# Stores of squared activations moved three products back in one issue queue, and three loads moved ahead

## The chip, the cores and the metric

The kernel runs on one core of a Trainium2 chip. The core has a matrix engine (TensorE, PE in the profile), which reads its operands from on-chip memory (SBUF) and adds into eight banks of a second memory (PSUM), and three engines for elementwise work: VectorE (DVE), ScalarE (ACT) and GpSimd (POOL). SyncE (SP) computes nothing: its queue issues the transfers (DMA) between SBUF and main memory. An engine takes its instructions strictly in order and stops at the first one that has to wait for another engine or for a transfer. The metric is the device time of one execution in microseconds.

## The reference

Attention with a threshold, and behind it a feed-forward network:

```
scores = q k^T / 8;  keep scores >= rowmax - tau;  softmax;  x = weights v      # 8 x 8 heads, 576 x 64
h = maximum(x @ w_in, 0)            # x 4608 x 512, w_in 512 x 2048
out = (h * h) @ w_out               # w_out 2048 x 512
```

All results are float32. The change lies in the feed-forward part, in its first layer `h * h`.

## The kernel before

**Three stages.** The attention comes first (to about 492 us) and leaves x transposed in main memory. The first layer (to about 881 us) computes squares g = max(x w_in, 0)^2 and stores them in main memory (`gT`). The output layer loads them again and multiplies by w_out. Tokens come in nine steps of 512.

**Products.** Both layers multiply with a scheme of seven products for eight, used twice: an outer index m runs over `OUTER = (1, 2, 6, 7, 4, 5, 3)` and, in each m, seven inner products, so that a pass has 49 products. I number them 0 to 48 in a pass; m = 1 has 0 to 6, m = 2 has 7 to 13, and so on. Each product goes into a PSUM bank and is then added into running sums: by DVE alone, or by DVE into one of six places (tag `t`) and from there by POOL (`add`, `final`). The m = 2, 4, 5 and 3 each finish four tiles of g (tag `o`, a ring of eight places); I call them block 2, 4, 5 and 3. So a place of `o` is written again two blocks later.

**Passes.** There are nine passes over the 49 products (`PASSES`): pass 0 for step 0, passes 1 to 6 for the pairs of steps (1, 2), (3, 4), (5, 6) with half of the columns each, passes 7 and 8 for steps 7 and 8. Passes 1 to 6 work on 256 tokens at once (L1000), the others on 128 (L817).

**What goes on beside the products.** `tick` (L1041) follows every product; what it emits stands in the engines' queues in that order, though an engine that is free may run ahead. It does, in this order:
- `chain_out`: weight chains for the second layer. A chain loads 256 KB of raw blocks of w_out (L1298), takes four differences of them on POOL six to nine products later (`minus`, L122) and stores the result (L1303) ten products behind its load. Chains begin at products 6, 12, 18, 24, 36 and 45 of each pass, and use two SBUF places in turn: a chain's load waits until the store of the chain before the last has landed.
- `before_x` (L921), in passes 0, 2, 4 and 6: loads the next steps' x from main memory (`load_x`, L838), by the table `BEFORE_X`: `(i, at): (part, slot)`, i counting the m's in their order and `at` the products in it. The slots are those of the steps now in work, each free once PE has read it for the last time; slot `None` is a place among x's sums. The first sum of the new x (from product 21 on) subtracts what lies in `None` from slot 2: ACT copies one operand into PSUM (`sum_v`, L856), and DVE subtracts (L122) one product later.
- `squares_due`: when a tile of g has been complete for six products (ten for block 3), ACT makes its Relu and its Square (L969, L970) and, at once, `square` puts its stores into SP's queue: one of 256 KB (L973) in a pass over one step, two of 128 KB (L976) in a pass over two.

SP's queue thus holds chain loads and stores, x loads and stores of squares in the order in which `tick` emits them. At the start of pass 8 the output layer's first loads (L1082) join it, and reloads of weights (L1225) follow.

Of the kernel before, what the change touches and what calls it, by code (L numbers as in the profile page):

```python
# [48 lines left out]
def kernel(  # L49
# [25 lines left out]
    nc = tc.nc  # L75
# [9 lines left out]
    BANK = 512  # L85
# [9 lines left out]
    gT = [[dram.tile([P, BANK], FP32, name=f"g{n}_{j}") for j in range(16)] for n in range(NSTEP)]  # L95
# [79 lines left out]
    raws, parts, asked_for = {}, {}, set()  # L175
# [336 lines left out]
    for g in range(2, 2 * len(pairs)):  # L512
        two, x = divmod(g - 4, 4)
# [300 lines left out]
    def by_tiles(to, lhs, rhs, start, stop):  # L814

        for cols in (ds(0, HALF), ds(HALF, HALF)):
            nc.tensor.matmul(to[cols], lhs[:, cols], rhs, start=start, stop=stop, skip_group_check=True)  # L817
# [68 lines left out]
    def part_x(steps, k, m, count=None):  # L886

        of = slice((steps[0] + 1) % 2, (steps[0] + 1) % 2 + len(steps))
        ms = slice(m - 1, m - 1 + count) if count else m - 1
        if k in (1, 7, 2, 3):  # L890
            return places_x[:, of, ms, k in (2, 3), k in (7, 3), :]
        return sums_x[:, of, (5, 6, 4).index(k), ms, :]
# [8 lines left out]
    def outer_x(steps, op, o, x, y):  # L901

        return [lambda n=n: sum_v(op, slot_x(n, o), slot_x(n, x), slot_x(n, y)) for n in steps]
# [9 lines left out]
    def ask_x(steps, m, slot):  # L913

        (part,) = [(a, c) for a, c in XPARTS if AT_B[a][c] == m]
        for n in steps:
            load_x(n, [part], slot_x(n, slot))

    BEFORE_X = {(1, 0): (1, 1), (1, 6): (7, None), (2, 0): (3, 2), (3, 6): (2, 2), (6, 0): (3, 5)}

    def before_x(steps, i, at):  # L921

        if (i, at) in BEFORE_X:
            ask_x(steps, *BEFORE_X[i, at])
        turned_ = lambda: outer_x(steps, minus, 6, 2, None)
# [23 lines left out]
        }  # L949
        return work.get((i, at), list)()  # L950

    LATER = {3: 4}
    waiting, half_made = deque(), []

    def advance_x():
# [7 lines left out]
    squares, clock = deque(), {"n": 0}  # L963
    def hidden_bank():
        return banks.tile([P, BANK], FP32, tag="b", bufs=6, name="ph")

    def square(n, j, o):

        nc.scalar.activation(out=o, in_=o, func=AF.Relu)  # L969
        nc.scalar.activation(out=o, in_=o, func=AF.Square)  # L970
        steps, h = n
        if h is None:
            nc.sync.dma_start(out=gT[steps[0]][j][:, :].rearrange("p (k t) -> p k t", k=4), in_=o)  # L973
            return
        for s_, step in enumerate(steps):
            nc.sync.dma_start(  # L976
                out=gT[step][j][:, ds(h * BANK // 2, BANK // 2)].rearrange("p (k t) -> p k t", k=2),
                in_=o.rearrange("p (k s) t -> p k s t", s=2)[:, :, s_, :],
            )

    def squares_due(wait):

        if squares and squares[0][0] + wait <= clock["n"]:
            square(*squares.popleft()[1:])

    def hidden_layer(n, also):

        steps, h = n
        of = prepared.pop(steps[0], None)
        tile4 = lambda tag, bufs: hid.tile([P, 4, NQ], FP32, tag=tag, bufs=bufs)  # L990
        bank = lambda: hidden_bank()[:, :].rearrange("p (k t) -> p k t", k=4)
        temp = lambda name: tile4("t", 6)
        U2, U3 = {}, {}

        for m in OUTER:

            def product(to, k, more):
                if h is not None:
                    for j in range(2):
                        nc.tensor.matmul(  # L1000
                            to[:, 2 * j : 2 * j + 2, :], W_IN[m, k][:, ts(2 * h + j, P)], part_x(steps, k, m),
                            start=(not more and j == 0), stop=True, skip_group_check=True,
                        )
                    return
                x = of[k][:, m - 1, :] if of else part_x(steps, k, m)[:, 0, :]
                for j in range(4):
                    by_tiles(to[:, j, :], W_IN[m, k][:, ts(j, P)], x, not more and j == 0, True)

            def add(to, c, other, more, t=None):

                if other is None:
                    plus(nc.vector, to, c, more)
                else:
                    plus(nc.gpsimd, to, t, more)

            def final(ab, c, other):
                if m == 1:
                    U2[ab] = tile4("u", 12)
                    if other is None:
                        nc.scalar.copy(U2[ab], c)  # L1020
                    else:
                        plus(nc.vector, U2[ab], c, other)
                    return
                t = None
                if other is not None:
                    t = temp("t")
                    plus(nc.vector, t, c, other)
                if m == 6:
                    add(U2[ab], c, other, U2[ab], t)
                elif m == 7:  # L1030
                    U3[ab] = tile4("u", 12)
                    add(U3[ab], c, other, U2[ab], t)
                else:
                    o = tile4("o", 8)
                    add(o, c, other, U3[ab] if m in (4, 5) else U2[ab], t)
                    if m == 5:
                        add(U2[ab], c, other, U2[ab], t)
                    row, col = {2: (0, 0), 4: (1, 0), 5: (1, 1), 3: (0, 1)}[m]
                    squares.append((clock["n"] + LATER.get(m, 0), n, 4 * (2 * row + ab[0]) + 2 * col + ab[1], o))

            def tick(at):  # L1041
                clock["n"] += 1
                also(m, at)
                squares_due(6)

            inner(product, copy, temp, bank, final, tick)


# [130 lines left out]
    with tc.manual_schedule():  # L1179
# [127 lines left out]
        for n, (steps, h) in enumerate(PASSES):  # L1307
# [14 lines left out]
            def also(m, at):  # L1322
                i = OUTER.index(m)
                convert_out(n, 7 * i + at)
                chain_out(n, 7 * i + at)
                if ahead:
                    waiting.extend(before_x(ahead, i, at))
                if 0 < n < 8 and h != 1:
                    waiting.extend(within_x(group, i, at))
                advance_x()  # L1330
                if not last:
                    return
                spread(work.get(i, []), at)
                reload_due(7 * i + at)

            hidden_layer((steps, h), also)
        for n in range(NSTEP):
            more = n + 1 < NSTEP

            def work_of(i):  # L1340

                work = [] if i == 6 else inner_sums(n, OUTER[i + 1])
                if (n, i) == (0, 0):
                    work += outer_sums(0, 6, (1, 2)) + outer_sums(0, 5, (4,)) + outer_sums(0, 6, (4,))
                if (n, i) == (0, 1):
                    work += outer_sums(0, 7, (1, 2, 4))
                if (n, i) == (0, 2):
                    work += outer_sums(0, 3, (1, 2, 4))
                if more and i == 4:
                    work += outer_sums(n + 1, 5) + outer_sums(n + 1, 7, (7, 1))  # L1350
                if more and i == 5:
                    work += outer_sums(n + 1, 6) + outer_sums(n + 1, 7, (2, 4))
                if more and i == 6:
                    work += outer_sums(n + 1, 3) + inner_sums(n + 1, 1)
                return work

            def also(m, at):
                i = OUTER.index(m)
                if n == 0:
                    reload_due(49 + 7 * i + at)  # L1360
                if n == 0 and (i, at) in ((2, 0), (3, 0)):
                    load_g(1, [(m_, k) for m_ in ((7,) if i == 2 else (4, 1, 2)) for k in K_ORDER])
                if n and more and (i, at) == (0, 0):
                    load_g(n + 1, [(m_, k) for m_ in KINDS[0:2] for k in K_ORDER])
                if at == 0:
                    work[0] = work_of(i)
                spread(work[0], at)
                if at > 4:
                    squares_due(-max(LATER.values()))
                if at == 2:  # L1370
                    ask()
                if at == 6:
                    if n and more and i == 0:
                        load_g(n + 1, [(7, k) for k in K_ORDER])
                    if n and more and i == 1:
                        load_g(n + 1, [(4, k) for k in K_ORDER])

            work = [None]
            output_layer(n, also)
# [37 lines left out]
```

## Time and profile before

| what | us |
|---|---|
| three runs, median (lowest to highest) | 1272.59 (1271.4 to 1273.39) |
| the profiled execution, its own time | 1272.82 |
| span of that execution, first to last instruction | 1271.0 |
| PE busy | 1249.6 |
| DVE, POOL, ACT busy | 989.3, 983.2, 844.4 |
| first layer, nine passes | about 491.9 to 881.5 |

The page's times are of one execution on the chip. A row of a timeline gives start, duration, engine, line, operation, output and input, how many instructions it joins and, in brackets, how long the engine stood idle before it and what ended that. Rows of SPq are transfers being issued; they land some microseconds later. A row of windows gives a stretch, its length, and busy time (with the count of instructions) of PE, weight loads, DVE, ACT and POOL, then the clock granted to PE as a share of the full one, the busy share of the transfer engines, and GB/s.

### The profile page before, as it was taken

Reading aid. Unit: us, or ns where it says so; the run is one execution under the profiler, and the core shown is the slowest. Engines: PE = TensorE matmul, PEld = TensorE weight load, DVE = VectorE, ACT = ScalarE, POOL = GpSimd, SP = SyncE. Lnnn points to the kernel's source line nnn. Section 1 sums busy time; section 2 is a strip of 40 time slices with the busy share of each in tenths; the row PEclk is TensorE's granted clock in tenths of the full one; section 3 lists DMA queues with packets and bytes.
Section 4 is the critical chain, followed back from the end, with each engine's and each line's share of the span. In section 5 each row is a group of like instructions: output and inputs, shape, how many; then the busy total and the mean of one; then the engine's idle time right before and its main releaser. Section 6 shows DMA issues by size and latency. Waiting matters only on the chain.

```text
span 1271.0 us, 55420 instructions
## 1 busy us (share of the span) xinstructions
PE 1249.6 (98%) x22991; PEld 1093.1 (86%) x22991; DVE 989.3 (78%) x2385; ACT 844.4 (66%) x1536; POOL 983.2 (77%) x1070
## 2 busy tenths in 40 slices
PE   8999999999999999999999999999999999999998
PEld 5777777777777778987888888999999999999998
DVE  6999999999999996886887878867746654665463
ACT  6999999999999994665765866675524432443240
POOL 3989998877776543987897988868787878787776
PEclk9999999999999999999999999999999999999999
DMA  7666676434333323658768768679755225522511
GB/s 184 149 166 157 168 193 187 118 93 105 89 83 87 79 60 99 199 161 230 200 190 226 217 172 232 192 260 374 278 163 168 78 97 163 168 69 101 167 36 35
DMA packets 291450, 196.81 MB, mean 155 GB/s; under 512 B 100096, under 2 KB 252160, under 8 KB 291200
## 3 DMA queue, kind: packets, MB, share of 16 engines
q1 hardware_dynamic: 289888, 192.87, 53.0%
q8 instruction: 181, 2.97, 1.0%
q14 instruction: 69, 0.57, 0.1%
q10 hardware_dynamic: 1312, 0.41, 0.1%
HBM read 120.85 MB, written 72.35 MB: 152 GB/s over the span
## 4 chain that ended last, share of the span: by engine, by line
PE 74%; DMA 2%; POOL 2%; ACT 1%; issue 1%; DVE 1%; SPq 0%; DVEq 0%; ACTq 0%; POOLq 0%
PE po L817 30%; PE ph L1000 14%; PE ph L817 10%; PE sc L560 7%; PE sc L458 6%; PE pt L402 4%; POOL arena L125 1%; PE sc L541 1%; PE sc L422 1%; DMA w<-arena 1%; DMA arena<-w 1%; POOL arena L122 1%; ACT arena L969 1%; PE sc L402 0%; DVE arena L125 0%
## 5 line engine op out<-in xcount | busy, mean ns | idle before, releaser
L125 POOL TENSOR_TENSOR arena<-arena 128x512 f32<-128x512 f32 (+1 forms) x314 | 378.7, 1224 | 118.6 <-DVE arena L125 105.2
L817 PE MATMUL po<-wall,arena 128*64 128x128 f32 x7056 | 385.5, 273 | 0.8 <-ACT arena L812 0.8
L817 PEld LDWEIGHTS po<-wall,arena 128*64 128x64 f32 x7056 | 385.2, 137 | 1.0 <-ACT arena L812 1.0
L125 DVE TENSOR_TENSOR arena<-ph,arena 128x512 f32<-128x512 f32 x378 | 254.9, 689 | 78.1 <-PE ph L1000 31.9
L122 POOL TENSOR_TENSOR arena<-arena 128x128 f32<-128x128 f32 (+1 forms) x322 | 265.9, 827 | 30.9 <-DMA arena<-w 14.4
L1000 PE MATMUL ph<-arena,wall 128*128 128x256 f32 x1176 | 257.7, 381 | 2.8 <-DVE arena L125 2.6
L1000 PEld LDWEIGHTS ph<-arena,wall 128*128 128x128 f32 x1176 | 223.6, 191 | 36.8 <-DVE arena L125 6.3
L125 DVE TENSOR_TENSOR arena<-po,arena 128x128 f32<-128x128 f32 x378 | 108.0, 290 | 159.4 <-PE po L817 153.9
L491 DVE SCALAR_TENSOR_TENSOR arena<-arena 128x576 f32<-128x576 f32 x288 | 226.0, 821 | 0.4 <-ACT arena L486 0.4
L486 ACT ACTIVATE arena<-arena 128x576 f32<-128x576 f32 x288 | 213.5, 779 | 13.2 <-DVE arena L476 13.1
L476 DVE TENSOR_SCALAR_CACHE_REDUCE arena<-sc 128x576 f32<-128x576 f32 x288 | 203.4, 753 | 15.9 <-issue 5.7
L856 ACT COPY c<-arena 128x512 f32<-128x512 f32 (+1 forms) x295 | 168.8, 578 | 69.9 <-DVE arena L122 37.5
L458 PE MATMUL sc<-arena 64*64 64x512 f32 (+1 forms) x2304 | 178.1, 413 | 5.8 <-ACT arena L551 1.4
L560 PE MATMUL sc<-arena 64*64 64x128 f32 (+1 forms) x5760 | 165.8, 261 | 1.1 <-ACT arena L551 0.5
L122 DVE TENSOR_TENSOR arena<-arena,c 128x512 f32<-128x512 f32 x235 | 154.5, 666 | 12.0 <-ACT c L856 6.6
L560 PEld LDWEIGHTS sc<-arena 64*64 64x64 f32 x5760 | 150.4, 133 | 4.8 <-issue 1.0
L551 ACT COPY arena<-pt 128x1024 f32<-128x1024 f32 x143 | 144.9, 1013 | 3.3 <-PE pt L402 2.6
L458 PEld LDWEIGHTS sc<-arena 64*64 64x64 f32 x2304 | 76.6, 133 | 70.4 <-issue 44.2
L812 ACT COPY arena<-po 128x128 f32<-128x128 f32 x63 | 16.6, 264 | 177.6 <-PE po L817 174.8
L817 PE MATMUL ph<-arena,wall 128*64 128x128 f32 x2352 | 129.2, 273 | 0.6 <-DVE arena L709 0.6
L817 PEld LDWEIGHTS ph<-arena,wall 128*64 128x64 f32 x2352 | 128.3, 137 | 1.4 <-issue 1.0
L483 POOL TENSOR_SCALAR arena<-arena,tau_p 128x2 f32<-128x2 f32 x144 | 83.3, 579 | 55.6 <-DVE arena L476 42.2
(55 smaller groups left out, 1140.4 us busy)
## 6 DMA issues: line engine op xcount, KB each, us to landing
arena<-g SPq DMA_DIRECT2D x144, 256.0 KB, 5.0
g<-arena SPq DMA_DIRECT2D x192, 128.0 KB, 2.9
w<-arena SPq DMA_DIRECT2D x60, 256.0 KB, 3.2
wall<-w SPq DMA_DIRECT2D x49, 256.0 KB, 5.2
g<-arena SPq DMA_DIRECT2D x48, 256.0 KB, 4.2
arena<-w SPq DMA_DIRECT2D x44, 256.0 KB, 3.4
arena<-in_v_dram SPq DMA_DIRECT2D x32, 288.0 KB, 4.0
out_dram<-arena SPq DMA_DIRECT2D x70, 128.0 KB, 2.7
```

Of the source, the lines that this page charges most:

```text
L122: e.tensor_tensor(out=out, in0=x, in1=y, op=ALU.subtract)
L125: e.tensor_tensor(out=out, in0=x, in1=y, op=ALU.add)
L458: made = nc.tensor.matmul(sc[at, ds(to, count)], lhs, kT[rows, ds(at_k, count)], start=True, stop=True)
L476: made = nc.vector.tensor_scalar(out=s[:, j, :], in0=sc[:, ds(at, S)], scalar1=1.0, scalar2=None, op0=ALU.mult, op1=ALU.min, accum_out=nmx ...
L483: nc.gpsimd.tensor_scalar(out=thr, in0=nmx, scalar1=tau_p[:, :], scalar2=None, op0=ALU.add)
L486: nc.scalar.activation(out=w[:, :, j, :], in_=of(j), func=AF.Exp, bias=nmx[:, j : j + 1], scale=-1.0)
L491: nc.vector.scalar_tensor_tensor(out=w[:, :, j, :], in0=of(j), scalar=thr[:, j : j + 1], in1=w[:, :, j, :], op0=ALU.is_le, op1=ALU.mult, a ...
L551: touch(kind, copy_by(joined(to), whole(pt, 0, count)), at, 2 * BANK, m)
L560: made = nc.tensor.matmul(sc[ds(u * D, D), ds(5 * j * BANK + row, count)], loaded_v[i][rows, (c - (u != j)) % CH, :], wT[m][rows, ds(weigh ...
L817: nc.tensor.matmul(to[cols], lhs[:, cols], rhs, start=start, stop=stop, skip_group_check=True)
L856: nc.scalar.copy(c, y)
L1000: nc.tensor.matmul(to[:, 2 * j : 2 * j + 2, :], W_IN[m, k][:, ts(2 * h + j, P)], part_x(steps, k, m), start=(not more and j == 0), stop=Tr ...
```

## The change

The stores of squares are no longer emitted with the square. They are kept in a list with the clock (the count of products) at the square, and `stores_due(LATE)`, called in every tick behind `also` and ahead of `squares_due`, emits those that are three products old. Before a place of `o` is written again, any store still kept for it is emitted first. In the output layer the clock goes on, with stores one product old in step 0, and all that are left after it. Three entries of `BEFORE_X` move: part 1 into slot 1 from the tick of product 7 to that of product 6, part 7 into `None` from 13 to 11, part 3 into slot 2 from 14 to 13.

```diff
-    BEFORE_X = {(1, 0): (1, 1), (1, 6): (7, None), (2, 0): (3, 2), (3, 6): (2, 2), (6, 0): (3, 5)}
+    BEFORE_X = {(0, 6): (1, 1), (1, 4): (7, None), (1, 6): (3, 2), (3, 6): (2, 2), (6, 0): (3, 5)}
...
-    LATER = {3: 4}
+    LATER, LATE = {3: 4}, 3
...
         if h is None:
-            nc.sync.dma_start(out=gT[steps[0]][j][:, :].rearrange("p (k t) -> p k t", k=4), in_=o)
+            to = gT[steps[0]][j][:, :].rearrange("p (k t) -> p k t", k=4)
+            kept.append((clock["n"], made_number(o), [(to, o)]))
             return
+        parts = []
         for s_, step in enumerate(steps):
...
+            parts.append((to, o.rearrange("p (k s) t -> p k s t", s=2)[:, :, s_, :]))
+        kept.append((clock["n"], made_number(o), parts))
...
+    def stores_due(wait, before=0):
+
+        while kept and (kept[0][0] + wait <= clock["n"] or kept[0][1] < before):
+            for to, from_ in kept.popleft()[2]:
+                nc.sync.dma_start(out=to, in_=from_)
...
+                    stores_due(LATE, len(hidden_made) - 7)
                     o = tile4("o", 8)
+                    hidden_made.append(o)
...
                 also(m, at)
+                stores_due(LATE)
                 squares_due(6)
...
+                clock["n"] += 1
+                stores_due(1 if n == 0 else 0)
```

In SP's queue of passes 1 to 6 this gives the following order (stores of squares by their block; a block has eight stores of 128 KB, so "2 of block 2" is one tile):

```
before: chain load 12, x loads, 2 of block 2, chain store 16, 4 of block 2, chain load 18, 2 of block 2, chain store 22, chain load 24
after:  chain load 12, x loads, chain store 16, chain load 18, 8 of block 2, chain store 22, chain load 24
```

The numbers are the products at which they are emitted. The order of instructions on PE, DVE, ACT and POOL stays as it was.

More of the change, by code (lines that the diff above doesn't have):

```diff
@@ L972, in square, with made_number @@
         if h is None:
-            nc.sync.dma_start(out=gT[steps[0]][j][:, :].rearrange("p (k t) -> p k t", k=4), in_=o)
+            to = gT[steps[0]][j][:, :].rearrange("p (k t) -> p k t", k=4)
+            kept.append((clock["n"], made_number(o), [(to, o)]))
             return
+        parts = []
         for s_, step in enumerate(steps):
[L976 to L979, printed above, removed]
+            to = gT[step][j][:, ds(h * BANK // 2, BANK // 2)].rearrange("p (k t) -> p k t", k=2)
+            parts.append((to, o.rearrange("p (k s) t -> p k s t", s=2)[:, :, s_, :]))
+        kept.append((clock["n"], made_number(o), parts))
+    hidden_made, kept = [], deque()
+    def made_number(o):
+        return next(i for i, x in enumerate(hidden_made) if x is o)
+    def stores_due(wait, before=0):
+        while kept and (kept[0][0] + wait <= clock["n"] or kept[0][1] < before):
+            for to, from_ in kept.popleft()[2]:
+                nc.sync.dma_start(out=to, in_=from_)
     def squares_due(wait):
```

## The prediction

> **What bounds the kernel now.** First the page's busy times, then the busy times of the nine passes of the hidden layer by window, then the waits of PE and of SP's queue, last the timelines around the one long wait. The waits of SP's queue are those between 540 and 950 us.
>
> ```profile
> span 1271.0 us, 55420 instructions
> PE 1249.6 (98%) x22991; PEld 1093.1 (86%) x22991; DVE 989.3 (78%) x2385; ACT 844.4 (66%) x1536; POOL 983.2 (77%) x1070
> ...
> 534.80:577.60 42.80, 42.80 (x197) 37.08 (x197) 34.96 (x57) 30.13 (x55) 38.10 (x47) 1.00 0.64 184
> 577.60:624.50 46.90, 44.33 (x198) 38.22 (x197) 32.77 (x50) 27.67 (x51) 37.11 (x47) 0.96 0.71 198
> 667.30:709.90 42.60, 42.60 (x197) 37.14 (x197) 32.54 (x51) 27.09 (x50) 35.43 (x45) 1.00 0.77 213
> ...
> PE ph L1000 <- DVE arena L125: 2.6, 1, 2.6
> PE po L817 <- ACT arena L812: 0.8, 1, 0.8
> ...
> SPq L1303 <- POOL arena L122: 62.0, 29, 4.3
> SPq L973 <- ACT arena L970: 20.2, 15, 9.0
> SPq L976 <- ACT arena L970: 14.0, 24, 2.0
> ```
>
> PE is busy 98% of the span. The windows are passes 1, 2 and 4: a pass over two steps takes 42.6 to 42.8 us and PE is never idle in it, but pass 2 takes 46.9. That is all this change can win: 46.9 - 42.8 = 4.1 us, 0.32%. SP's queue waits 62.0 us for POOL (results of the weight chains, L1303) and 34.2 us for ACT (squares to be stored, L973, L976). POOL, not PE, is the engine with the next least room: 38.1 of 42.8 us.
>
> ```profile
> 586.30 0.46 SPq L1298 DMA_DIRECT2D arena<-w  x1
> ...
> 593.41 0.49 SPq L1298 DMA_DIRECT2D arena<-w  x1
> 594.00 2.04 SPq L838 DMA_DIRECT2D arena<-xT  x4
> ...
> 599.77 1.31 ACT L856 COPY c<-arena 128x512 f32<-128x512 f32 x2 [2.52 <-DMA arena<-xT]
> ...
> 601.31 0.69 DVE L122 TENSOR_TENSOR arena<-arena,c 128x512 f32<-128x512 f32 x1 [3.03 <-DMA arena<-xT]
> ...
> 602.66 29.58 PE L1000 MATMUL ph<-arena,wall 128*128 128x256 f32 x126 [2.57 <-DVE arena L125]
> ...
> 602.00:604.00 2.00, 1.34 (x3) 1.17 (x4) 1.87 (x5) 0.00 (x0) 1.74 (x4) 0.60 0.55 163
> 604.00:606.00 2.00, 2.00 (x6) 1.55 (x6) 1.31 (x3) 0.00 (x0) 0.77 (x1) 0.54 0.54 149
> ...
> 885.00:890.00 5.00, 4.50 (x82) 4.50 (x84) 3.50 (x9) 4.08 (x9) 3.95 (x4) 1.00 1.04 390
> ```
>
> The stall of pass 2: four x loads go out at 594.0; the sum of x (L122) starts at 601.31, when the third has landed; DVE's next sums free the bank that PE waits for, and PE resumes at 602.66 after 2.57 us. The granted clock then falls to 0.60 and 0.54 for four microseconds, which is the rest of the 4.1. PE resumes 1.35 us after the sum starts, so PE would not have stopped had the sum started 2.57 us sooner, at 598.74: that is 21.1 us into the pass.
>
> **The change, part by part.** No instruction is added or removed on any engine, and the order on PE, DVE, ACT and POOL is the old one. What moves is the order in SP's queue, which issues one after the other and stops at the first that has to wait. So no place in the program makes a store "later" by three products in time; it makes it later by what now stands ahead of it. The price of a place is
>
> ```profile
> 570.56 6.53 SPq L976 DMA_DIRECT2D g<-arena  x12
> ```
>
> 6.53 / 12 = 0.54 us.
>
> (a) The x loads. In pass 2 the old queue has, behind the chain load at 586.30 (L1298, product 6), 12 issues and then the load that the sum needs. The new one has 14: the loads for slot 1 and for the free place (`None`) move up, but the two stores of block 3's first square, ahead of 586.30 before, now come behind it. The third of the four loads (some 595.1 in the row of 594.00) is thus two places later, not sooner: 1.1 us at the price above, against which stand the waits for ACT that go. The rows bound it: had SP no wait at all from 586.30 on, 15 x 0.54 = 8.1 us puts it at 594.4, 0.7 sooner; at the old pace, (595.1 - 586.3) / 13 = 0.68, it goes out 10.2 us behind, 1.4 later. I take +0.5 for the stall, a little over the middle, since the waits of SP that a landing transfer ends stay. In passes 4 and 6 the same two places are lost:
>
> ```profile
> 687.84 0.68 DVE L122 TENSOR_TENSOR arena<-arena,c 128x512 f32<-128x512 f32 x1
> ...
> 773.38 0.69 DVE L122 TENSOR_TENSOR arena<-arena,c 128x512 f32<-128x512 f32 x1
> ```
>
> Passes 4 and 6 begin at 667.3 and 752.6, so PE's limits are 688.4 and 773.7: room of 0.6 and 0.3. A load that landed at most at these starts, 1.1 later, costs PE up to 0.5 and 0.8. I take 0.5 for both together, since the landings themselves may be earlier.
>
> (b) The stores of block 2's squares. They were spread around the chain load of product 18; now all eight stand between that load and the chain store of product 22.
>
> ```profile
> 690.13 0.36 SPq L1298 DMA_DIRECT2D arena<-w  x1
> 690.58 1.00 SPq L976 DMA_DIRECT2D g<-arena  x2
> 691.63 0.54 SPq L1303 DMA_DIRECT2D w<-arena  x1
> 694.85 0.36 SPq L1298 DMA_DIRECT2D arena<-w  x1
> ...
> 697.25 0.99 POOL L122 TENSOR_TENSOR arena<-arena 128x128 f32<-128x128 f32 x2
> ...
> 732.53 0.97 SPq L976 DMA_DIRECT2D g<-arena  x2
> ...
> 775.92 0.97 SPq L976 DMA_DIRECT2D g<-arena  x2
> ...
> 740.06 0.46 POOL L122 TENSOR_TENSOR arena<-arena 128x128 f32<-128x128 f32 x1 [0.64 <-DMA arena<-w]
> ```
>
> The chain load of product 24 writes the place that the store of product 22 reads, so it waits for that store to land (694.85 behind 691.63), and POOL begins with it as soon as it is there (second half of the row 697.25; idle 0.64 in pass 5). Of the old stores four were hidden in the wait for the chain store of product 16, and two cost 1.0. Now eight cost 8 x 0.54 = 4.3, and the wait ahead of 690.13 stands empty: POOL's sums come 3.3 us later in passes 4, 5 and 6. What is late next is DVE: it writes each partial sum into one of six places that POOL must have read, and this reserve is already used up at the end of a pass:
>
> ```profile
> 578.24 0.69 DVE L125 TENSOR_TENSOR arena<-ph,arena 128x512 f32<-128x512 f32 x1 [0.67 <-POOL arena L125]
> ...
> 710.76 0.69 DVE L125 TENSOR_TENSOR arena<-ph,arena 128x512 f32<-128x512 f32 x1 [0.20 <-POOL arena L125]
> ...
> 753.02 0.69 DVE L125 TENSOR_TENSOR arena<-ph,arena 128x512 f32<-128x512 f32 x1 [0.45 <-POOL arena L125]
> ...
> 796.08 0.69 DVE L125 TENSOR_TENSOR arena<-ph,arena 128x512 f32<-128x512 f32 x1 [0.23 <-POOL arena L125]
> ```
>
> This sum and two more (three at 0.69, which overlap a little: 1.9 us) come ahead of the sixth product of the next pass, which begins 5 x 0.873 = 4.4 us into it. With 3.3 added: 710.76 + 3.3 + 1.9 = 716.0 against 709.9 + 4.4 = 714.3, a stall of 1.7; 758.2 against 757.0, 1.2; 801.3 against 799.7, 1.6. Together 4.5 us. In pass 1 the store of product 22 waited for POOL anyway:
>
> ```profile
> 555.24 0.44 SPq L1298 DMA_DIRECT2D arena<-w  x1
> ...
> 558.10 0.36 SPq L1303 DMA_DIRECT2D w<-arena  x1
> ```
>
> 2.9 us, against 0.45 + 4.3 = 4.8 now: 1.9 later, 578.24 + 1.9 + 1.9 = 582.0 against 582.0, no stall. I take pass 3 like pass 1, and pass 2 at nothing, since its own stall gives POOL time. The ends for (b): 0, if POOL turns out to have room, and 4.5 plus the clock.
>
> (c) The clock. A wait of 2.57 us cost 1.5 more by the clock; one of 0.8 (row 885: clock 1.00) cost nothing. The new stalls of 1.2 to 1.7 lie between, nearer to 0.8: I take nothing, with 4.5 (three times 1.5) as the other end. "TensorE: Matmul & The Clock Gate" of the Trainium skill (section Why this matters for your kernels) would have the clock hold through gaps under some 3 us; by that the new stalls cost no clock, as I take it, but the rows 602 and 604 show it falling after 2.57, so the measurement decides and the other end stays.
>
> (d) Stores of blocks 4, 5 and 3. Block 4's keep their place behind the chain load of product 36. Block 5's go behind the chain store of product 46, and their places are rewritten by block 2 of the next pass: 581.36 (that store) + 8 x 0.54 lands well before product 59; if that cover went, POOL would wait. At the end of pass 7 three stores go behind 16 loads; POOL is not short of time there. The output layer's stores go one product later; PE's only wait there (0.8) is for ACT. All at nothing.
>
> Sum: 0.5 + 0.5 + 4.5 = 5.5 us on the profiled execution's 1272.82, so 1278.3; the median of the three runs lies 0.2 below that execution, so 1278.0 us.
>
> **The rivals.** (1) Faster: SP, no longer held by squares, issues the loads 2.6 us sooner, the sum of pass 2 starts by 598.74, and POOL's reserve hides (b). For it: 34.2 us of waits for ACT; against it: the third load's two lost places. The price is the whole 4.1: 1272.6 - 4.1 = 1268.5. "DMA: Bandwidth & Descriptors" (Rules for kernel authors) speaks for this rival: issue the DMA early, wait late. Here the early issue holds for two of the three places only. (2) Nothing much: (b) is hidden and (a) alone counts, 1272.6 + 1.0 = 1273.6. For it: DVE's waits for POOL are under 0.7 and PE shows none. (3) Worse: (b) as reckoned, and the clock falls after each of the three stalls: 1278.0 + 4.5 = 1282.5.
>
> **How the numbers follow.** My forecast 0.52, (1) 0.20, (2) 0.14, (3) 0.14. Two runs can be told apart from about 0.2%, 2.5 us. Faster 0.20, same 0.12 (most of rival 2), slower 0.68. The likeliest case alone reaches from 1274 (half of b) to 1282; the range reaches up to rival 3 and down to half of the stall of pass 2 gone: 1270.0 to 1284.0.
>
> **What would show it.** In the profile after: in passes 4 to 6 eight stores in a row between the chain load of product 18 and the chain store of product 22, POOL idle for a chain load some 3 us longer at product 30, DVE waiting for POOL at the ends of these passes, and PE waits of 1 to 2 us just into passes 5, 6 and 7, where there are none now. Pass 2 keeps a wait of about 3 us. Wrong, if pass 2 takes 43 us or the passes after it stay at 42.7.

## The result, and the profile after

The changed kernel takes 1291.55 us (median, 1289.25 to 1291.79) against 1272.34 for the kernel before: a ratio of 1.0147, 95% interval 1.0129 to 1.0164. It is slower, as forecast, but by 19.2 us and not by 5.4; 1291.55 lies above the range.

Views of the changed kernel: the span from its page, the windows of passes 2, 4 and 6 with two microseconds inside pass 2, and the waits between 530 and 900 us (total, times, longest).

```profile
span 1287.4 us, 55410 instructions
...
575.20:625.70 50.50, 45.97 (x197) 39.06 (x197) 33.54 (x52) 28.22 (x50) 38.15 (x47) 0.93 0.69 192
604.00:606.00 2.00, 2.00 (x6) 1.57 (x5) 1.10 (x2) 0.00 (x0) 1.92 (x4) 0.50 1.04 306
668.50:718.10 49.60, 45.76 (x198) 38.94 (x197) 33.06 (x51) 28.23 (x51) 37.64 (x47) 0.93 0.69 192
761.60:811.00 49.40, 45.14 (x200) 37.84 (x200) 33.14 (x52) 28.79 (x51) 38.01 (x47) 0.97 0.71 197
...
POOL arena L122 <- DMA arena<-w: 32.8, 14, 4.5
DVE arena L122 <- DMA arena<-xT: 13.4, 3, 4.9
PE ph L1012 <- DVE arena L125: 12.6, 5, 4.4
DVE arena L125 <- POOL arena L125: 7.1, 7, 1.8
```

The same two lines of POOL and DVE in the kernel before:

```profile
POOL arena L122 <- DMA arena<-w: 14.1, 11, 3.4
...
DVE arena L125 <- POOL arena L125: 1.8, 5, 0.7
```

The loss sits in the three passes that load the next x. Pass 2 grew from 46.9 to 50.5 us, pass 4 from 42.6 to 49.6, pass 6 (as long as pass 4 before) to 49.4: 3.6 + 7.0 + 6.8 = 17.4 us. DVE waits in each of them for an x load (13.4 us in three waits), PE waits 12.6 us for DVE where it waited 2.6, and after each long wait the granted clock stands at 0.50, for 6.8 us in passes 2 and 4 and for 3.4 us in pass 6, which makes most of the other 7.4. (The spans differ by 16.4 us: passes 5 and 7 add some 1.4, and in this execution the first layer begins 2.5 us earlier than in that of before.)

The chain that leads there is best read in SP's queue, in passes 3 and 4 (L1313 chain load, L1318 chain store, L991 stores of squares, L838 x loads). First the changed kernel:

```profile
646.21 5.21 SPq L991 DMA_DIRECT2D g<-arena  x8
651.51 0.44 SPq L1318 DMA_DIRECT2D w<-arena  x1
654.47 0.36 SPq L1313 DMA_DIRECT2D arena<-w  x1
...
657.63 0.45 POOL L122 TENSOR_TENSOR arena<-arena 128x128 f32<-128x128 f32 x1 [3.20 <-DVE arena L122]
...
670.51 1.53 POOL L122 TENSOR_TENSOR arena<-arena 128x128 f32<-128x128 f32 x3
...
673.71 0.36 SPq L1318 DMA_DIRECT2D w<-arena  x1
674.17 5.58 SPq L991 DMA_DIRECT2D g<-arena  x8
679.84 0.68 SPq L1318 DMA_DIRECT2D w<-arena  x1
680.57 0.50 SPq L1313 DMA_DIRECT2D arena<-w  x1
...
688.72 0.49 SPq L1313 DMA_DIRECT2D arena<-w  x1
689.32 2.12 SPq L838 DMA_DIRECT2D arena<-xT  x4
...
695.08 1.22 PE L1012 MATMUL ph<-arena,wall 128*128 128x256 f32 x2 [3.72 <-DVE arena L125]
```

and the kernel before (L1298 chain load, L1303 chain store, L976 stores of squares):

```profile
648.04 0.46 SPq L1303 DMA_DIRECT2D w<-arena  x1
650.79 0.36 SPq L1298 DMA_DIRECT2D arena<-w  x1
...
666.98 1.53 POOL L122 TENSOR_TENSOR arena<-arena 128x128 f32<-128x128 f32 x3
...
670.17 0.36 SPq L1303 DMA_DIRECT2D w<-arena  x1
670.63 4.07 SPq L976 DMA_DIRECT2D g<-arena  x4
674.79 0.42 SPq L1303 DMA_DIRECT2D w<-arena  x1
675.30 0.52 SPq L1298 DMA_DIRECT2D arena<-w  x1
...
680.40 0.53 SPq L1298 DMA_DIRECT2D arena<-w  x1
680.97 4.47 SPq L838 DMA_DIRECT2D arena<-xT  x8
```

Passes 3 and 4 begin 1.2 us later in the changed kernel, so 1.2 is to be taken off each difference. The eight stores of block 2 at 646.21 put chain store 22 from 648.04 to 651.51 and chain load 24 from 650.79 to 654.47 (2.5 later within the pass). POOL stands 3.20 us before its difference at 657.63; the row names DVE as the releaser, but that chain load landed at 657.57. POOL is still 2.3 us late at the pass end (670.51), so chain store 46 goes out 2.3 later (673.71). Behind it now stand the eight stores of block 5 (674.17), where four stood before, and chain store 6 with chain load 6 is 4.1 later (680.57). Then come block 3's stores, chain load 12 is 7.1 later (688.72), and behind it the load of slot 2 begins at 689.32. In the kernel before it is the second half of the eight at 680.97, from 683.2 on (680.97 + 4 x 4.47 / 8): 4.9 us sooner within the pass. Of these 4.9 us, 2.3 are POOL's lateness (block 2), some 1.7 come with the four more stores between chain stores 46 and 6 (block 5), and the last 0.9 between chain load 6 and the load of slot 2, where two more stores of block 3 now stand. PE stops for 3.72 us.

### The profile page after: what moved, and what is told of

It is laid out like the page before. It is cut to its first block, busy times and chain, and to the rows that moved or that the text cites. A ratio compares the mean times of both kernels' runs of the same rounds, so it can differ in the third digit from the quotient of the medians.

```text
span 1287.4 us, 55410 instructions
## 1 busy us (share of the span) xinstructions
PE 1256.9 (98%) x22991; PEld 1095.7 (85%) x22991; DVE 990.1 (77%) x2385; ACT 845.0 (66%) x1536; POOL 981.7 (76%) x1070
## 5 line engine op out<-in xcount | busy, mean ns | idle before, releaser
L125 POOL TENSOR_TENSOR arena<-arena 128x512 f32<-128x512 f32 (+1 forms) x314 | 378.1, 1222 | 109.8 <-DVE arena L125 90.1
L125 DVE TENSOR_TENSOR arena<-ph,arena 128x512 f32<-128x512 f32 x378 | 255.6, 689 | 84.9 <-PE ph L1012 31.3
L1012 PE MATMUL ph<-arena,wall 128*128 128x256 f32 x1176 | 265.5, 388 | 13.3 <-DVE arena L125 12.6
L1012 PEld LDWEIGHTS ph<-arena,wall 128*128 128x128 f32 x1176 | 226.6, 194 | 51.9 <-DVE arena L125 19.6
L125 DVE TENSOR_TENSOR arena<-po,arena 128x128 f32<-128x128 f32 x378 | 107.9, 289 | 159.5 <-PE po L817 154.0
L122 DVE TENSOR_TENSOR arena<-arena,c 128x512 f32<-128x512 f32 x235 | 154.6, 666 | 23.5 <-DMA arena<-xT 13.4
```

The lines of the kernel that those rows point to most:

```text
L122: e.tensor_tensor(out=out, in0=x, in1=y, op=ALU.subtract)
L125: e.tensor_tensor(out=out, in0=x, in1=y, op=ALU.add)
L1012: nc.tensor.matmul(to[:, 2 * j : 2 * j + 2, :], W_IN[m, k][:, ts(2 * h + j, P)], part_x(steps, k, m), start=(not more and j == 0), stop=Tr ...
```

## The experiments

Two explanations stood at first. **POOL late**: block 2's stores hold chain store 22 and chain load 24, POOL is late in the odd passes and with it, in the next pass, every chain store in SP's queue and the x loads behind them. **Places**: block 5's and block 3's stores, moved behind chain store 46 and ahead of the x loads, hold SP by themselves. A third, **table**, blames the moved loads.

All times are set against runs of the kernel before that were taken beside them (medians 1272.07 to 1273.27). Where blocks are given their own lateness, the edit is this, with the numbers of `LATE` as named; 0 issues the store with its square, and the other calls of `stores_due` count accordingly:

```diff
-    LATER, LATE = {3: 4}, 3
+    LATER, LATE = {3: 4}, {2: 0, 4: 3, 5: 3, 3: 3}
...
+        late = LATE[{(0, 0): 2, (1, 0): 4, (1, 1): 5, (0, 1): 3}[j // 8, j // 2 % 2]]
+        kept.append((clock["n"] + late, made_number(o), parts))
+        if not late:
+            stores_due(0)
```

**1. The moved loads alone.**

```diff
-    BEFORE_X = {(1, 0): (1, 1), (1, 6): (7, None), (2, 0): (3, 2), (3, 6): (2, 2), (6, 0): (3, 5)}
+    BEFORE_X = {(0, 6): (1, 1), (1, 4): (7, None), (1, 6): (3, 2), (3, 6): (2, 2), (6, 0): (3, 5)}
```

> The kernel before with the three moved entries of BEFORE_X alone; every store of a square is issued with its square, as before. Theory 'POOL late' (the eight stores of block 2 hold chain store 22 and chain load 24, POOL falls behind in passes 1, 3 and 5, and chain stores 46 and 6 of the next pass, with the x loads behind them, go late) and theory 'places' (the stores of blocks 5 and 3, now behind chain store 46 and ahead of the x loads, hold SP): the x loads find the old queue ahead of them, so passes 4 and 6 stay at 42.6 to 43, pass 2 stays between 43 and 47.5, time 1268.5 to 1273. Theory 'table' (the moved loads themselves do the harm): passes 2, 4 and 6 at 49 to 50, time 1287 to 1292.

Measured 1271.23 against 1273.27 us, ratio 0.9989 (0.9978 to 1.0000). The windows of passes 2 and 4:

```profile
578.70:622.50 43.80, 43.18 (x197) 36.87 (x196) 32.61 (x51) 27.10 (x49) 35.31 (x45) 1.00 0.73 205
665.30:707.90 42.60, 42.59 (x198) 37.14 (x197) 32.53 (x51) 27.14 (x49) 35.36 (x45) 1.00 0.75 211
```

Pass 2 takes 43.8 us where it took 46.9, and pass 4 has not moved. "Table" falls: the moved loads do no harm. In this execution they win 3.1 us of the 4.1 that were there to win, in the medians 2.0, with an interval that just reaches no gain. Nor is the gain there in every execution: in the profile of run 7 below, with the same loads moved, PE waits 2.23 us in pass 2, and the pass takes 46.6 us.

**2. The late stores alone** (the changed kernel with the old table, the diff of 1 reversed).

> The changed kernel with the old table BEFORE_X: stores three products late, loads where they were. 'POOL late' and 'places': passes 2, 4 and 6 still 49 to 51, since slot 2's load goes out behind the same queue and behind chain load 12 as well, time 1289 to 1296. 'Table': close to the kernel before, 1272 to 1276.

1293.06 us, ratio 1.0152 (1.0133 to 1.0171): the whole loss is the stores'.

**3. Block 2 prompt** (`LATE` 0 for block 2, 3 for 4, 5 and 3; moved loads).

> The changed kernel, but the stores of block 2 are issued with their squares, as before; blocks 4, 5 and 3 stay three products late and the loads stay moved. 'POOL late': chain load 24 goes out as before, passes 4 and 6 come back to 42.6 to 44, pass 2 to 43 to 48, time 1271 to 1277. 'Places': nothing changes for the x loads, passes 4 and 6 stay at 48 to 50, time 1285 to 1292. Half and half would show as 1277 to 1285.

1282.25 us, ratio 1.0066 (1.0048 to 1.0085): half and half. PE's waits at the first x sum are down to 1.29 us in pass 4 and 1.57 in pass 6; in pass 2 it is still 4.28, against 4.43 in the changed kernel.

**4. Only block 2 late** (`LATE` 3 for block 2, 0 for the others; old table).

> The kernel before, with only block 2's stores three products late; blocks 4, 5, 3 and the loads as before. 'POOL late': most of the loss, passes 4 and 6 at 47 to 50, time 1284 to 1292. 'Places': 1272 to 1275, with POOL's waits for chain load 24 some 3 us longer but no wait of PE in passes 4 and 6. The prediction's step (b) would give 1272.6 + 4.5 = 1277.1, with waits of PE of 1 to 2 us just inside passes 5, 6 and 7.

1281.32 us, ratio 1.0063 (1.0045 to 1.0082), +8.0 us, between the two forecasts for "POOL late" and step (b), and above "places". Its queue in pass 3 (L997 squares, L1324 chain store, L1319 chain load), the waits between 530 and 900 us, and PE at the x sum of pass 4:

```profile
644.99 5.37 SPq L997 DMA_DIRECT2D g<-arena  x8
650.45 0.44 SPq L1324 DMA_DIRECT2D w<-arena  x1
653.40 0.36 SPq L1319 DMA_DIRECT2D arena<-w  x1
...
POOL arena L122 <- DMA arena<-w: 26.4, 15, 3.4
DVE arena L125 <- POOL arena L125: 6.4, 9, 1.8
...
691.47 0.70 PE L1018 MATMUL ph<-arena,wall 128*128 128x256 f32 x2 [1.39 <-DVE arena L125]
```

The first half of the chain is there without the second: eight stores ahead of chain store 22, POOL's waits for chain loads up from 14.1 to 26.4 us, DVE's for POOL from 1.8 to 6.4. PE waits at the x sums (1.96, 1.39 and 0.49 us in passes 2, 4 and 6, together 3.84 where it was 2.57) and again at the ends of these passes (3.05 us together, where the kernel before lists none), but not at the sixth product of a next pass. So more of what block 2 adds by itself comes at the pass ends than at the x loads.

**5, 6, 7. Block 5, block 3 or block 4 alone late**, each with the moved loads and the others prompt.

> Loads moved as in the change, and of the stores only block 5's three products late. Block 5's eight stores then stand between chain store 46 and chain store 6 instead of six of them ahead of it. Theory 'places': chain load 6 goes out about 10.5 us into passes 4 and 6 (8.2 before, 9.4 with block 2 alone prompt), the load of slot 2 behind it at about 18.4 (limit about 17), PE waits 1 to 2 us at the first x sum of passes 4 and 6, time 1276 to 1281. If block 3's or block 4's late stores do it instead: passes 4 and 6 at 42.6 to 43, time 1269.5 to 1273.

> Loads moved as in the change, and of the stores only block 3's three products late: two of them go from ahead of chain store 6 to behind chain load 6, so the load of slot 2 keeps its distance (16 us into the pass). 'Places' by this count: passes as with the loads alone, 1269.5 to 1273. If block 3's stores ahead of the x loads are the cause of the 9 us that blocks 4, 5 and 3 cost together: 1277 to 1282.

> Loads moved as in the change, and of the stores only block 4's three products late. Their place against the chain loads and stores hardly changes (they stay between chain store 34 and chain load 45 of the same pass): 1269.5 to 1273, as the loads alone, passes 4 and 6 at 42.6 to 43. If late stores harm wherever they stand: 1275 or more.

Block 5: 1282.1 us, ratio 1.0082 (1.0059 to 1.0106), a little above its forecast. Block 3: 1275.68, ratio 1.0024 (1.0010 to 1.0037), between its two forecasts. Its count had taken two stores off the way to chain store 6; but in pass 6 that one stood 2.5 us waiting for POOL, so it did not go out sooner, and the two stores, now ahead of the load of slot 2, come on top. Block 4: 1270.74, ratio 0.9988 (0.9975 to 1.0002), as the loads alone. Against the loads alone (-2.0 us) that is +12.0, +5.6 and -0.3 us. The queue with block 5 late, at the start of pass 4, and what follows:

```profile
674.23 0.36 SPq L1324 DMA_DIRECT2D w<-arena  x1
674.68 6.41 SPq L997 DMA_DIRECT2D g<-arena  x10
681.18 0.46 SPq L1324 DMA_DIRECT2D w<-arena  x1
...
695.69 0.48 PE L1018 MATMUL ph<-arena,wall 128*128 128x256 f32 x1 [1.90 <-DVE arena L125]
```

Ten stores (block 5's eight, two of block 3's) stand between chain stores 46 and 6; nothing of block 2 is involved. Block 4, whose stores pass no chain store and no x load, costs nothing that can be told from noise. In pass 3 its stores go out behind chain load 36 as they did before (twelve in a row from 658.64, 659.04 in the kernel before), because SP stands at chain stores 28 and 34 until then; so this run does not yet show that a later store is harmless, run 9 does. Blocks 5 and 3 together with 4 (run 3: +11.0 over the loads alone) cost less than 12.0 + 5.6. With both late the two stores of block 3 are no longer ahead of chain store 6, which would explain it; it was not tested apart.

**8. Block 2 late with the moved loads**, and **9. block 2 late by nine products** with them (the others prompt).

> Loads moved as in the change, and of the stores only block 2's three products late. If the costs add: 1271.2 (loads alone) + 8 = 1279, chain load 6 about 10.3 us into passes 4 and 6, the load of slot 2 about 18.2, PE waits of 1 to 2 us at the first x sum. If the moved loads take the harm of block 2's stores away: 1271 to 1274.

> Loads moved as in the change, and of the stores only block 2's late, by nine products instead of three: they then stand behind chain store 22 and chain load 24 instead of ahead of them. 'POOL late' (what harms is standing ahead of chain store 22): nothing of the 8 us is left, chain load 24 goes out as early as before or earlier, 1268.5 to 1272, which is this kernel's chance to be the fastest. If lateness as such harms (places of squares, transfers bunched behind): 1276 or more.

With three products 1280.55 us, ratio 1.0071 (1.0045 to 1.0096), as if the costs added: +10.5 us over the loads alone, and with the +11.0 of run 3 that is 21.5, against 19.2 + 2.0 = 21.2 for the changed kernel. With nine products 1271.7, ratio 0.9999 (0.9980 to 1.0018). The queue of pass 3 with nine:

```profile
646.76 0.36 SPq L1324 DMA_DIRECT2D w<-arena  x1
649.06 0.36 SPq L1319 DMA_DIRECT2D arena<-w  x1
649.51 4.50 SPq L997 DMA_DIRECT2D g<-arena  x8
```

The same eight stores, later still but now behind chain store 22 and chain load 24 instead of ahead of them, cost nothing against the kernel before, and some 1.7 us over the loads alone, which is within the noise. So lateness as such is harmless here; the place in the queue is how block 2's stores do harm. It is not a better kernel than the loads alone.

**10, 11. x loads issued from ACT's queue**, in the changed kernel and in the one with the loads alone:

```diff
-    def load_x(n, parts=XPARTS, slot=None):
+    def load_x(n, parts=XPARTS, slot=None, queue=nc.sync):
...
-                nc.sync.dma_start(out=to[:, :, ds(done, m)], in_=src)
+                queue.dma_start(out=to[:, :, ds(done, m)], in_=src)
...
-            ask_x(steps, *BEFORE_X[i, at])
+            ask_x(steps, *BEFORE_X[i, at], queue=nc.scalar)
```

> The changed kernel with all its late stores, but the x loads of BEFORE_X are issued from ACT's queue, so no store and no chain load stands ahead of them. If the x loads held in SP's queue are the way by which the late stores cost PE time: no wait of PE at the first x sum of passes 2, 4 and 6, and 14 to 20 of the 19 us come back, 1271 to 1277. If POOL's lateness reaches PE by itself (step b of the prediction: DVE waits for places of t), what stays is 4.5 us or more at the pass ends, 1276 to 1280. If neither, 1285 to 1293.

> The kernel with the moved loads alone, its x loads also issued from ACT's queue. Passes 4 and 6 have no stall to lose, pass 2 has at most 1.0 us left (43.8 against 42.8); ACT, busy two thirds of its time, takes about 10 issues more per pair of passes. If ACT has the room: 1269 to 1272, as the loads alone or 1 us better. If ACT's copies come late behind the issues or behind a load's wait for PE: PE waits for ACT in passes 0, 2, 4 and 6, 1274 to 1282.

1301.84 us, ratio 1.0224 (1.0205 to 1.0244), above every forecast made for it, and 1282.45, ratio 1.0071 (1.0049 to 1.0093), just above the forecast for late copies of ACT. ACT in pass 2 of the first:

```profile
589.46 0.63 ACT L969 ACTIVATE arena<-arena 128x512 f32<-128x512 f32 x1 [5.36 <-DMA g<-arena]
...
593.03 6.46 ACTq L838 DMA_DIRECT2D arena<-xT  x4
599.59 0.58 ACT L812 COPY arena<-ph 128x512 f32<-128x512 f32 x1 [5.99 <-DMA arena<-xT]
```

ACT stands still 5.36 us until a store of squares has landed, and 5.99 us behind four x loads. In the program as it is built each transfer waits until the one eight before it has landed, counted over all queues. The trace shows it: the transfers of both queues carry eight landing counters in turn, and the three x loads that ACT's queue issued from 587.38 on waited for the counters of stores that SP had issued at 585.18, 586.25 and 586.83; these landed at 587.30, 588.24 and 588.82. So an x load in ACT's queue still waits for the stores that SP issues late, and ACT's copies wait behind it. The move didn't separate the x loads from the stores, and the question stayed open. (The counters are not what held chain store 22 in pass 3 of the changed kernel: its counter was free at 651.16, and issuing the last of the eight stores took until 651.41, right ahead of its 651.51.)

**12, 13. Without the loads** (e12 and e13 in the expectations). The entries `(1, 4)` and `(1, 6)` of the new table are left out of the changed kernel, and `(1, 6)` and `(2, 0)` of the old table out of the kernel before.

> The changed kernel, leaving out the loads of part 7 into the free place and of part 3 into slot 2 (the sums of x then use what lies there, so the squares of steps 1 to 8 are not the reference's; all sums and products are still made). Everything late stays late, but the first x sum has no transfer to wait for. If those loads are the way to PE: no wait of PE at the first x sum, passes 2, 4 and 6 at 42.6 to 44.5, 1270 to 1276. If POOL's lateness reaches PE by itself (step b, through the places of t): 4 us or more stay above the next kernel, e13. If neither: 1285 or more.

> The kernel before with the same two loads left out, the zero line for e12: the stall of pass 2 goes, passes at 42.6 to 43, 1268 to 1270. e12 minus e13 is what the late stores cost without these loads: 0 to 2 if the loads are the only way to PE, 4.5 or more if step (b) holds.

1278.15 us, ratio 1.0038 (1.0023 to 1.0052), above the 1270 to 1276 forecast if the loads were the only way, and 1268.67, ratio 0.9970 (0.9952 to 0.9987), as expected. PE has no wait at the first x sum in either. The waits between 530 and 900 us, first of the changed, then of the kernel before, both without the loads:

```profile
POOL arena L122 <- DMA arena<-w: 29.2, 18, 3.4
DVE arena L125 <- POOL arena L125: 13.2, 21, 1.8
PE ph L1012 <- DVE arena L125: 2.7, 6, 0.7
```

```profile
POOL arena L122 <- DMA arena<-w: 4.9, 4, 2.0
DVE arena L125 <- POOL arena L125: 1.2, 3, 0.7
```

With the x loads out of the way the late stores still cost 1278.15 - 1268.67 = 9.5 us: POOL waits 29.2 us for chain loads, DVE 13.2 us for places that POOL has to free, and PE stops for a moment in passes 1 to 5, at their products 41 to 48 above all: 2.7 us for DVE and 1.5 for ACT in the waits that are listed, the rest in shorter stops and in slower products behind each. The most is lost in passes 2 (46.8 against 42.4 us) and 4 (44.4 against 42.5). So step (b)'s way to PE exists. In the changed kernel itself little of it shows (PE's waits of 0.39 and 0.25 us at the ends of passes 5 and 6), presumably because PE already stands still at the x sums and POOL catches up meanwhile. Both ways are fed by the same late chain loads, and closing one opens the other; what the loads add on top is 1291.55 - 1278.15 = 13.4 us, less some 4 that leaving them out wins in the kernel before too.

## Why the prediction went wrong

**Direction, and the place of the trouble: right.** The eight stores in a row, chain load 24 late (2.5 us within pass 3, 3.3 forecast), POOL late behind it: as step (b) had them, and run 9 shows that their place ahead of chain store 22 is the cause.

**Step (b), where the lateness goes: wrong.** It was followed to DVE's six places and to PE at product 5 of the next pass, 4.5 us. No wait of that size came there. It should also have been followed to the next thing that waits for POOL in SP's queue: chain store 46 and chain store 6, with the x loads behind them. Block 2 alone cost 8.0 us, at x sums and, the larger part, at the ends of the passes that load x; so the way over DVE's places was not wrong in kind, but it reaches PE in other passes and at other products. The prediction lists that SP's queue waits 62.0 us for POOL, and does not follow it; it was the way by which POOL's lateness gets into the queue. The price of a place was low too: eight stores took 5.2 and 5.6 us (646.21, 674.17), not 4.3.

**Step (d), block 5 at nothing: the largest miss.** The cover named was that the places of `o` are rewritten late enough. That nearly holds: in the changed kernel POOL's sums (L125) wait 2.1 us in all for stores of squares, 0.5 before. What stands behind those eight stores in the queue, namely chain store 6, chain load 6 and all the x loads, does not come into step (d). It measured +12.0 us over the loads alone. Block 4 at nothing was right.

**Step (a), mis-sized.** Two stores of block 3 come ahead of the slot 2 load, as reckoned; forecast +1.0 over the kernel before, measured +3.6 (interval 1.3 to 4.7) in run 6. It also supposed that chain load 6 starts when it did before; in the changed kernel it starts 4.1 us later, and steps (a), (b) and (d) share one margin, 0.3 to 0.6 us in passes 4 and 6. Only step (a) was priced against it, as if it had the whole.

**Step (c), the clock at nothing: wrong** for the waits that came. They were 3.7 to 4.4 us, not 1.2 to 1.7, and their passes lost about 3 us more each. For waits of 1.2 to 1.6 us the step was right: none of that length lowered the clock in any run.

**Rival (1) was right for the loads alone** (run 1): the stall of pass 2 nearly went. Its price of 4.1 us was an upper bound; it got 2.0 in the medians, hardly more than the noise. The combination lost it, because the stores undo what the table gains. Rival (3), stalls with the clock, was the nearest in kind, at 1282.5 still 9 us short.

The signs named beforehand: the eight stores, the longer waits of POOL and those of DVE for POOL (7.1 us instead of 1.8) came; waits of PE just into passes 5, 6 and 7 did not; pass 2 kept its wait, at 4.4 instead of about 3 us.

## What to carry to other kernels

When stores move within an in-order issue queue, list for each moved group what it now stands ahead of, and follow that to its consumer, round the loop if need be: here stores delay a load, the load delays POOL, POOL delays a store in the same queue, and that delays the next loads. Price the sum of all moved groups against the one margin of the tightest consumer behind them, not each group by itself. Stores that nobody waits for belong behind the loads and the stores that free a buffer (run 9), and another engine's queue is no way out when transfers wait for each other's landing over all queues (runs 10 and 11).

## What the runs showed of the hardware

**The clock after a short gap.** The granted clock changes only at the steps of a fixed grid. In the changed kernel it is 0.50 from 601.71 to 608.54, from 693.87 to 700.70 and from 789.45 to 792.86; from one of these moments to the next it is 6.83, 85.33, 6.83, 88.75 and 3.41 us, which is 2, 25, 2, 26 and 1 steps of 3.413 us. Every run's trace has such a grid, each time at another place against the start of the kernel. Two examples, cut at the grid: with block 5 late PE resumes at 695.69 after 1.90 us (shown above), with block 3 late at 601.25 after 2.60.

```profile
693.22:696.63 3.41, 1.51 (x7) 0.96 (x6) 2.15 (x4) 0.00 (x1) 3.08 (x4) 1.00 1.05 299
696.63:700.04 3.41, 3.41 (x9) 2.75 (x9) 2.32 (x4) 0.00 (x0) 2.34 (x4) 0.50 0.83 239
```

```profile
596.15:599.57 3.42, 2.50 (x12) 1.87 (x10) 0.69 (x1) 0.68 (x2) 0.45 (x2) 1.00 0.91 265
599.57:602.98 3.41, 1.73 (x8) 1.50 (x9) 2.94 (x5) 0.00 (x0) 3.33 (x6) 1.00 0.84 249
602.98:606.39 3.41, 3.41 (x18) 3.00 (x17) 2.64 (x5) 2.24 (x5) 2.69 (x5) 1.00 0.81 230
```

Here the shorter gap costs clock and the longer one does not. The shorter gap lies in one step: PE is idle 3.41 - 1.51 = 1.90 us of it, and the next step runs at 0.50. The longer gap falls into two steps, with 0.92 and 1.69 us idle (3.42 - 2.50 and 3.41 - 1.73 with the rounding of the rows), and the clock stays at 1.00. PE's gaps over 1.1 us in the first layer of all the runs, the most that PE was idle in one step of the grid around each, and the clock in the next step:

| gap of PE, us | most idle in one step, us | clock |
|---|---|---|
| 1.12, 1.13, 1.19, 1.24, 1.29, 1.39, 1.46, 1.53, 1.56, 1.57 | 0.67 to 1.57 | 1.00 each |
| 2.01, 2.28, 2.36, 2.45, 2.60 | 1.60, 1.86, 1.63, 1.49, 1.69 | 1.00 each |
| 1.86, 1.90, 1.96, 2.23, 2.57 | 1.94, 1.90, 1.95, 2.22, 2.33 | 0.50 each |
| 3.08, 3.45, 3.72, 3.84, 4.03, 4.12, 4.28, 4.43, 4.80 | 2.19 to 3.41 | 0.50 each |

By length of the gap there is no order between 1.8 and 2.6 us; by the idle time in one step there is: up to 1.86 us nothing, from 1.90 us always. (The gap of 1.86 has another short one in its step.) The same holds for every step at full clock in all fifteen traces from 25 us on, 14 with a fall and some 5400 without. PE's ends are modelled, so 1.9 us is the limit as these traces count it.

The half clock then lasts one step if PE is idle at most 0.24 us in it (9 cases), and two if it is idle 0.74 us or more (5 cases), and so costs up to 1.7 or 3.4 us. In the kernel before, the stall of 2.57 us had 2.33 us in one step; where the grid lies can thus decide whether such a stall costs clock. That it makes part of the spread of repeated runs is likely, but was not tested.

"TensorE: Matmul & The Clock Gate" of the Trainium skill (section HAM oscillation — how this bites in real kernels) gives gaps of more than some 3.4 us as those to avoid. The five falls after 1.86 to 2.57 us show that shorter ones can cost clock too. In its section What's actually happening the same page of the Trainium skill has an activity window of about 3.4 us that runs freely, without regard to the kernel's start. The grid of 3.413 us agrees with that.

**Another issuing engine.** "DMA: Bandwidth & Descriptors" of the Trainium skill (section Issuing engines are not separate DMA queues) has it that issuing from several engines saves only the sequencer's time. Runs 10 and 11 agree that there was no more to win, and show that it can cost: against the same kernels with the x loads in SP's queue, 11.4 us more with prompt stores (+9.4 instead of -2.0) and 9.6 more with late ones (+28.8 instead of +19.2), with the waits of ACT shown above.
